# Batch 0 of an attention and channel-mix kernel in fp32 on TensorE, new planner costs, and one more tile in three rings

## The chip, the cores and the metric

The kernel runs on one core of a Trainium2 chip. A core has a matrix engine (TensorE, PE in the profile, with PEld for its weight loads), a vector engine (VectorE, DVE), an activation engine (ScalarE, ACT), a general engine (GpSimd, POOL), and a queue engine (SyncE, SP) that starts DMAs here. Each works through its own instructions in order and waits on semaphores. Data lie in SBUF, and matmuls write into eight PSUM banks. The metric is the time of one execution on the device in microseconds (us), as the median of several runs.

## The reference

```python
def _attn_ref(q, k, v, g_q, g_k):          # (8, 12, 448, 64) each
    q_n, k_n = (rmsnorm(q, g_q), rmsnorm(k, g_k))
    scores = 1.0 / np.sqrt(64) * np.matmul(q_n, k_n.transpose(0, 1, 3, 2))
    attn = np.exp(scores - np.max(scores, axis=-1, keepdims=True))
    attn = attn / (np.sum(attn, axis=-1, keepdims=True) + 1e-09)
    return np.matmul(attn, v)

def _moe_ref(x, mu_k, mu_r, w_k, w_v, w_r): # x (8, 448, 768), w_k 768x1024, w_v 1024x768, w_r 768x768
    xk = mu_k * x + (1.0 - mu_k) * x_prev   # x_prev: x moved by one token
    xr = mu_r * x + (1.0 - mu_r) * x_prev
    k = np.maximum(xk @ w_k, 0.0)
    return 1.0 / (1.0 + np.exp(-(xr @ w_r))) * (k * k @ w_v)
```

q, k, v and the result are fp32. The five weight inputs come as 64-bit floats.

## The kernel before

fp32 accuracy is had from f16 matmuls. Each operand is split into a high half (rounded to f16) and a low half (the rest, again in f16), and each product is three f16 matmuls: high x high, high x low, low x high.

**Attention.** Two heads make a pair, two pairs a unit `u`; a batch is 6 pairs or 3 units, and the tokens are 448 = 7 blocks of 64. `stats` (L568) and `preps` (L591) normalise q and k; for the first 6 units (`PE_T`) `turn` (L625) transposes them on PE as fp32 and ACT and DVE split the result into `stk`. `scores` (L709) runs over 7 groups per unit (168 in all): 6 groups of one pair and 128 tokens, and one corner group for the last 64 tokens of both pairs. A group writes two sc banks, one per head; the two heads stand in different halves of the array. `expo` (L744) finds the row maximum (DVE) and the exponential with its sum (ACT).

The probabilities then go one of two ways (`probs` L756, `probs_pe` L789). Ten groups, the odd ones below 21 (`PE_P`), go by PE: ACT writes the exponential to a `nat` tile as fp32, POOL scales it by 1/sum, PE transposes it as fp32 into sc banks, ACT copies out the high half and DVE the low half into `pT`. All others go by DMA: ACT and DVE split the scaled exponential straight out of the sc banks into a `nat` tile (`split` L813), and SP transposes that by DMA into `pT`. `attends` (L821) multiplies with v. `vprep` (L673) splits v into `vh` and `vl`, scaled by a power of two. `pT` has one place for even pairs and one for odd ones. The `nat` ring has 4 tiles; at the start it can borrow space in `xk`, which is why some `nat` tiles are named xk in the profile, and weight staging tiles kk.

**Channel mix.** `mix` (L871) makes xk and xr for a batch from 6 pairs (df on POOL, then DVE, split by ACT and POOL). `moe` (L992) then runs, per batch, the key products (mm<-xk with wk), squares them into `kk` (`square` L1051, ring kf), and the receptance and value products. `wload`, `weights` and `wsplit` (L896 to L931) bring in 20 weight tiles of 128 columns, decode them from 64-bit floats (POOL, ACT, DVE), find each column's scale through a product on PE and its diagonal (dg, DVE, and a true fp32 matmul with ones), and split them. Of batch 0, the key products may begin once all its pairs are mixed and all wk tiles are there, and the rest once all 20 tiles are done.

**The order.** All parts are generators that yield instructions. A list scheduler (`Plan.run` L300) holds a modelled clock for each engine, and takes the instruction with the earliest start less a priority. `Plan.emit` (L250) advances the clocks by modelled prices: `TR_COST` for a transposition on PE, constants for a DMA, and a rule that a DVE instruction with all operands in SBUF begins no sooner than 190 ns before POOL's last one ends. That order is the order on each engine; semaphores do the rest on the chip. A `Ring` (L329) hands out tiles of one shape.

All instructions are recorded by one helper (L256 in the profile), so groups are told apart by the tiles' names.

Of the kernel before, what the change touches and what calls it, by code (L numbers as in the profile page):

```python
# [74 lines left out]
Q_DVE = 1  # L75
PE_T = 6
SWITCH = 600
MODE = {"sc": 1, "t6": 2, "av": 3}
# [11 lines left out]
SC_KEEP = 2  # L90
TR_COST = 300
W_GAP = 10e3
# [4 lines left out]
DMA_SHARE = 1.0  # L97
PE_SLOW = 1.0
F64_EXP = 2.0 ** -112
F64_NEG = -2.0 ** 32  # L100
# [53 lines left out]
def in_psum(x):  # L154
    return "PSUM" in str(x.tensor.space)
# [37 lines left out]
class Plan:  # L193
    LAT = 35

    def __init__(self, tc):
        self.tc = tc
        self.clk = dict.fromkeys(("PE", "DVE", "ACT", "POOL", "SP"), 0.0)
        self.last, self.use, self.threads = {}, {}, []
        self.form, self.dma_free, self.pool_end, self.n = None, {"SP": 0.0, "ACT": 0.0}, 0.0, 0  # L200

# [48 lines left out]
    def emit(self, ops):  # L250
# [18 lines left out]
        elif ops[0].fn.__name__.startswith("dma"):  # L269
# [3 lines left out]
            if "transpose" in op.fn.__name__:  # L273
                w, iss, tot = n / 128 * 1.21, 1510, 4000
            else:
                w, iss, tot = n / 55, 600, 3300
            w, tot = w * DMA_SLOW, tot * DMA_SLOW
# [11 lines left out]
        else:  # L289
            op = ops[0]  # L290
            pace, dur = (x * OP_SLOW for x in price(op))
            if e == "DVE" and not any(in_psum(x) for x in op.kw.values() if isinstance(x, bass.AP)) and width(op.kw["out"]) > 2:
                s = max(s, self.pool_end - 190)
            self.clk[e] = s + pace
            if e == "POOL":
                self.pool_end = s + dur
            self.note(op, s + dur)
        self.n += 1

    def run(self):  # L300
        while self.threads:
            best, key = None, None
            for th in list(self.threads):
                if not isinstance(th[2], list):
                    if not th[2]():
                        continue
                    self.advance(th)
                    if th not in self.threads or not isinstance(th[2], list):
# [3 lines left out]
                wait = SWITCH if mode == 0 and self.form else 0  # L312
                k = max(self.clk[th[2][0].eng] + wait, th[3] + slack) - PS * (th[1]() if callable(th[1]) else th[1])
                if best is None or k < key:
                    best, key = th, k
# [13 lines left out]
class Ring:  # L329
    def __init__(self, pool, shape, dtype, name, n, plan):  # L330
        self.pool, self.shape, self.dtype, self.name, self.plan = pool, shape, dtype, name, plan
        self.free, self.of, self.lent = ["%s%d" % (name, k) for k in range(n)], {}, {}

# [11 lines left out]
    def get(self, early=False):  # L345
# [5 lines left out]
        if not isinstance(tag, str):  # L351
            self.of[id(tag)] = (tag, None, tag)
            return tag
        pool = self.pool() if callable(self.pool) else self.pool
        t = pool.tile(self.shape, self.dtype, name=tag, bufs=1)
# [33 lines left out]
def attn_moe_kernel(tc, q, k, v, g_q, g_k, mu_k, mu_r, w_k, w_v, w_r, out):  # L389
# [201 lines left out]
    def preps():  # L591
        for u in range(NQ):
# [4 lines left out]
            for n, t in enumerate(LD.pop(u)):  # L597
# [3 lines left out]
                if u < PE_T:  # L601
# [4 lines left out]
                    R["qk"].put(t)  # L606
                    yield from turn(w, X, n)
                    R["nat"].put(nat)
# [15 lines left out]

    def turn(w, X, n):  # L625
        for a0 in range(0, NT, 4):
# [14 lines left out]
            hi, lo = (X[:, n, o + a0:o + a0 + m, :] for o in (0, NT))  # L641
            if n == 0:
                yield A.activation(out=hi, in_=src, func=AF.Copy, scale=gc[:, 0:1])
# [21 lines left out]
    def vpreps():  # L665
        for i in range(NPAIR):
            st["vi"] = i
            yield from until(lambda: i in VF and st["tq"] >= GATE_V)
            vh = yield from R["vh"].get()
            vl = yield from R["vl"].get()  # L670
            yield from vprep(i, VF.pop(i), vh, vl)

    def vprep(i, vf, vh, vl):  # L673
# [4 lines left out]
        vs = small.tile([P, 2], F32, name="vs", bufs=4)  # L678
        yield A.activation(out=vh.bitcast(BF16), in_=vf, func=AF.Square, accum_out=vs[:, 0:1])
        pt = yield from banks["ot"].get()  # L680
        yield T.matmul(form=("v", 60), out=pt[:, 0:P], lhsT=vs[:, 0:1].bitcast(BF16)[:, 1:2].broadcast_to([P, P]), rhs=ident16, start=True, stop=True)
# [5 lines left out]
        yield V.tensor_scalar(out=iv.bitcast(I32), in0=sv.bitcast(I32), scalar1=-1.0, scalar2=float(0x7F000000), op0=ALU.mult, op1=ALU.add)  # L687
        yield A.activation(out=vh, in_=vf, func=AF.Copy, scale=sv)
        yield V.scalar_tensor_tensor(out=vl, in0=vf, scalar=sv, in1=vh, op0=ALU.mult, op1=ALU.subtract)
        VFREE.append(vf)  # L690
        VV[i] = vh, vl, iv
        if hp == NP - 1:
# [16 lines left out]
    def scores():  # L709
        for gi, (u, x, t0) in enumerate(groups):  # L710
            yield from until(lambda: u in TQ and len(banks["sc"].free) > (SC_KEEP if gi in PE_P else 1) and not st["zq"])
            tp = None
            if gi in PE_P:
                tp = yield from R["nat"].get(u < 3)
# [5 lines left out]
            both_pairs = t0 == NT - 1  # L720
            for m, (kl, ql) in enumerate(((0, 0), (0, 1), (1, 0))):
                for i in (2 * u + 1, 2 * u) if both_pairs else (2 * u + x,):
                    X = TQ[u]
                    for h in (1, 0):
# [3 lines left out]
                        ops.append(T.matmul(  # L728
                            form=("t6" if both_pairs else "sc", 3 * S / 2.368),
                            out=both[h][o:o + HD, 0:S] if both_pairs else both[h][:, 0:S],  # L730
                            lhsT=X[hs, 1, ql * NT + t0, o:o + HD] if both_pairs else X[hs, 1, ql * NT + t0 + i % 2, :],
                            rhs=X[hs, 0, kl * NT:(kl + 1) * NT, o:o + HD],
                            start=(m == 0), stop=(m == 2)))
            yield ops
# [21 lines left out]
    def probs(gi, both, sums, D, tp):  # L756
        u, x, t0 = groups[gi]
        yield from until(lambda: len(D) == 2 and st["g"] == gi)
        for i in (2 * u, 2 * u + 1) if t0 == NT - 1 else (2 * u + x,):
            if i not in PT:  # L760
                yield from until(lambda: PTFREE[i % 2])
                PTFREE[i % 2] = False
                PT[i] = PTQ[:, :, i % 2 * S:(i % 2 + 1) * S]
                CNT[i] = 0
# [24 lines left out]
    def probs_pe(u, x, t0, sums, tp):  # L789
# [8 lines left out]
        for a0 in range(0, NT, 4):  # L798
# [5 lines left out]
            src = z[:, 0:m * P].rearrange("p (a c) -> p a c", c=P)  # L804
            hi, lo = (PTQ[:, h + a0:h + a0 + m, c0:c0 + P] for h in (0, NT))
            yield A.copy(out=hi, in_=src)
            yield V.tensor_tensor(out=lo, in0=src, in1=hi, op=ALU.subtract)
            banks["sc"].put(z)
# [12 lines left out]
    def attends():  # L821
        for i in range(NPAIR):
# [5 lines left out]
            ops = []  # L828
            for j, (pl, hl, c) in enumerate(PASSES):
                for h in range(2):  # L830
                    ops.append(T.matmul(
                        form=("av", len(PASSES) * S / 2.368),
                        out=av[h * HD:(h + 1) * HD, 0:S],
                        lhsT=(vl if hl else vh)[:, NSL * h + c, :],
                        rhs=pT[:, NT * pl + (NSL - 1) * h + c, :],
                        start=(j == 0), stop=(j == len(PASSES) - 1)))
            yield ops
            PTFREE[i % 2] = True
            R["vh"].put(vh)
            R["vl"].put(vl)  # L840
            for lo, hi in ((0, NT),) if i % 2 == 0 else ((NT - 1, NT), (0, NT - 1)):
                o = 0 if i % 2 == 0 or lo else HD
                yield A.activation(out=x[:, 1 + lo:1 + hi, :].rearrange("p t c -> p (t c)"), in_=av[:, o:o + (hi - lo) * HD], func=AF.Copy, scale=iv)
            banks["ot"].put(av)
# [86 lines left out]
    def wsplit(nm, kt, c, ci, f):  # L931
# [178 lines left out]
```

## Time and profile before

| | |
|---|---|
| median of 3 runs | 1060.49 us (1059.37 to 1060.85) |
| the profiled execution, its own time | 1058.49 us |
| its span in the profile | 1056.7 us |
| PE busy | 925.9 us (88%), 6185 matmuls |
| DVE busy | 802.9 us (76%) |
| ACT busy | 770.7 us (73%) |
| POOL busy | 675.8 us (64%) |

The page cuts the span into 40 equal slices of 26.4 us; a digit is the busy share in tenths, PEclk the granted TensorE clock in tenths of full speed:

```profile
PE   1667666889988999998989999999899999999997
DVE  5888899898699688868997897959876898673100
PEclk9567878899999999999999999999999999999999
```

PE is at 60 to 70% in the slices of the first 180 us, at a reduced clock, and near full from then on. DVE is at 80 to 90% from the second slice. In rows of instruction groups, the numbers behind the bar are busy us and mean ns of one, then the idle time of the engine just before them and what ended it. An instruction's row begins with its start and its length in us.

### The profile page before, as it was taken

The numbers are of one execution on the slowest core, as the hardware profiler recorded it, in microseconds if no ns is written. First come the engines' busy times: TensorE is split into PE (matmuls) and PEld (weight loads), VectorE is DVE, ScalarE is ACT, GpSimd is POOL, SyncE is SP. The second block draws the span as 40 slices with busy tenths as digits, with TensorE's granted clock in tenths as the row PEclk, the third lists the DMA queues.
The fourth block names the chain that finished last, engine by engine and source line by source line (L and its number), as shares of the span: only waits on it lengthen the run. The fifth ranks groups of instructions, "written<-read, shape, count | busy, mean of one in ns | idle before, by whom it ended". The sixth has DMA issues, their size and how long they took to land. (4 is left out here: it accounts for less than half of the span.)

```text
span 1056.7 us, 19126 instructions
## 1 busy us (share of the span) xinstructions
PE 925.9 (88%) x6185; PEld 488.9 (46%) x6185; DVE 802.9 (76%) x2034; ACT 770.7 (73%) x1786; POOL 675.8 (64%) x716
## 2 busy tenths in 40 slices
PE   1667666889988999998989999999899999999997
PEld 1334323444544555454534455455445554455564
DVE  5888899898699688868997897959876898673100
ACT  3687877888679788877788787868787888773311
POOL 2575579655588576874698457857695569725711
PEclk9567878899999999999999999999999999999999
DMA  6865557876877899778976998679887898753011
GB/s 172 196 145 123 136 140 189 176 145 134 178 134 146 163 172 165 155 149 148 176 160 129 181 174 165 136 143 183 151 152 153 165 179 164 135 89 79 1 31 30
DMA packets 467108, 151.68 MB, mean 144 GB/s; under 512 B 438848, under 2 KB 463424, under 8 KB 467008
## 3 DMA queue, kind: packets, MB, share of 16 engines
q1 hardware_dynamic: 447472, 132.47, 66.1%
q10 hardware_dynamic: 19536, 18.00, 5.9%
q8 instruction: 48, 0.79, 0.3%
q14 instruction: 52, 0.43, 0.1%
HBM read 50.40 MB, written 11.01 MB: 58 GB/s over the span
## 5 line engine op out<-in xcount | busy, mean ns | idle before, releaser
L256 PE MATMUL mm<-wvh,kk 128*128 128x384 f16 x896 | 233.3, 326 | 0.5 <-DVE o L256 0.5
L256 ACT ACTIVATE sc<-sc,sums 128x448 f32<-128x448 f32 x316 | 192.2, 611 | 54.1 <-DVE sums L256 47.1
L256 DVE SCALAR_TENSOR_TENSOR nat<-sc,sums,nat 128x448 f16<-128x448 f32 x306 | 199.8, 676 | 37.0 <-ACT nat L256 35.3
L256 PE MATMUL mm<-xk,wkh 128*128 128x448 f16 x768 | 213.1, 359 | 9.7 <-DVE WSC L256 5.7
L256 ACT ACTIVATE nat<-sc,sums 128x448 f16<-128x448 f32 (+1 forms) x326 | 194.9, 646 | 25.8 <-DVE sums L256 10.4
L256 DVE TENSOR_REDUCE sums<-sc 128x1 f32<-128x448 f32 x336 | 193.6, 614 | 21.9 <-PE sc L256 21.3
L256 PE MATMUL mm<-wrh,xr 128*128 128x384 f16 x672 | 177.1, 326 | 0.0
L256 PEld LDWEIGHTS <-kk 128*128 128x128 f16 (+1 forms) x1362 | 129.5, 98 | 97.2 <-issue 15.6
L256 PE MATMUL sc<-stk 64*128 64x448 f16 (+1 forms) x1152 | 128.3, 369 | 34.4 <-DVE nat L256 19.4
L256 PE MATMUL mm<-wvl,kk 128*128 128x384 f16 x448 | 146.0, 326 | 0.0
L256 PE MATMUL mm<-xk,wkl 128*128 128x448 f16 x384 | 137.8, 359 | 0.0
L256 PE MATMUL ot<-pT,vh 128*64 128x448 f16 x768 | 122.4, 376 | 17.3 <-DMA pT<-nat 8.0
L256 PEld LDWEIGHTS <-xr 128*128 128x128 f16 x1008 | 95.6, 98 | 73.4 <-issue 13.1
L256 DVE SCALAR_TENSOR_TENSOR df<-x,bsc,df 128x448 f32<-128x448 f32 x96 | 108.3, 1137 | 25.3 <-POOL df L256 25.0
L256 PEld LDWEIGHTS <-wkh 128*128 128x128 f16 x768 | 72.8, 99 | 83.9 <-issue 25.5
L256 PE MATMUL mm<-wrl,xr 128*128 128x384 f16 x336 | 109.5, 326 | 0.0
L256 PEld LDWEIGHTS <-stk 64*128 64x128 f16 (+1 forms) x1152 | 43.5, 99 | 103.3 <-issue 68.5
L256 POOL TENSOR_TENSOR o<-o,bsc 128x384 f32<-128x384 f32 x48 | 43.8, 913 | 69.5 <-DVE o L256 57.0
L256 POOL TENSOR_TENSOR nat<-nat 128x448 f32<-128x448 f32 x46 | 53.9, 1171 | 50.6 <-ACT nat L256 45.4
L256 POOL TENSOR_TENSOR qk<-qk,ss 128x896 f32<-128x896 f32 x36 | 62.5, 1737 | 34.5 <-DVE ss L256 28.8
L256 DVE SCALAR_TENSOR_TENSOR o<-o,mm 128x384 f32<-128x384 f32 x56 | 30.6, 546 | 70.2 <-PE mm L256 70.2
L256 POOL TENSOR_TENSOR nat<-qk,nat 128x896 f16<-128x896 f32 x36 | 67.8, 1883 | 23.4 <-ACT nat L256 23.3
(141 smaller groups left out, 1632.6 us busy)
## 6 DMA issues: line engine op xcount, KB each, us to landing
out_dram<-o SPq DMA_DIRECT2D x56, 192.0 KB, 3.3
qk<-in_k_dram SPq DMA_DIRECT2D x46, 224.0 KB, 4.0
qk<-in_q_dram SPq DMA_DIRECT2D x108, 64.0 KB, 2.5
vf<-in_v_dram SPq DMA_DIRECT2D x96, 64.0 KB, 2.8
raw<-in_moe_w_v_dram ACTq DMA_DIRECT2D x12, 512.0 KB, 4.7
vf<-in_v_dram SPq DMA_DIRECT2D x96, 48.0 KB, 2.5
raw<-in_moe_w_r_dram ACTq DMA_DIRECT2D x12, 384.0 KB, 3.7
kk<-in_moe_w_k_dram ACTq DMA_DIRECT2D x8, 384.0 KB, 4.0
```

What stands on the lines that cost most here:

```text
L256: r = op.fn(op.kw["out"], op.kw["value"]) if op.fn.__name__ == "memset" else op.fn(**op.kw)
```

## The change

Four things change.

1. For the first three units (`U32 = 3`, which is batch 0) nothing is split. q, k, probabilities and v stay fp32, and each product is one fp32 matmul instead of three f16 ones. `whole` views a tile of two f16 halves as one fp32 tile. All 21 score groups of these units go by PE, so there are 11 more by PE and 11 fewer by DMA. The copies out of PSUM after a transposition go to ACT or DVE, whichever has the earlier modelled clock. v is used as it was loaded, but `vprep` still finds its scale, since the mix needs it.
2. Because `pT` now changes its format, pair 6 waits until both its places are free.
3. The planner: `TR_COST` 130 for 300, `ACC_GAP` 130 between accumulating ACT instructions, dearer DMA issues, and a rule on sharing between DVE and POOL that holds both ways.
4. After the weight staging pool is closed, the rings kf, df and nat get one tile more each (`LATE_BUFS`; kfx, dfx and natx in the rows). Two guards in `wsplit` make steps wait until values exist.

```diff
-TR_COST = 300
+U32 = 3
+TR_COST = 130
+ACC_GAP = 130
+LATE_BUFS = (("kf", 1), ("df", 1), ("nat", 1))
+def whole(ap):
+    c = ap.shape[-1]
+    return ap.rearrange("p a c -> p (a c)").bitcast(F32).rearrange("p (a c) -> p a c", c=c)
...
-                w, iss, tot = n / 128 * 1.21, 1510, 4000
+                w, iss, tot = n / 128 * 1.21, 1600, 4000
...
+            if e == "ACT":
+                acc = op.kw.get("accum_out") is not None
+                if acc and self.acc:
+                    s = max(s, self.clk[e] + ACC_GAP)
+                self.acc = acc
+            if e == "POOL" or e == "DVE" and not any(in_psum(x) for x in op.kw.values() if isinstance(x, bass.AP)) and width(op.kw["out"]) > 2:
+                for a, b in self.held["DVE" if e == "POOL" else "POOL"]:
+                    if a <= s < b - 190:
+                        s = b - 190
...
+            for name, n in LATE_BUFS:
+                R[name].grow(late_pool[0], n)
...
+            if u < U32:
+                dst = whole(X[:, n])[:, a0:a0 + m, :]
+                if plan.clk["ACT"] < plan.clk["DVE"]:
+                    yield A.activation(out=dst, in_=src, func=AF.Copy, scale=gc[:, 0:1]) if n == 0 else A.copy(out=dst, in_=src)
...
-            yield from until(lambda: u in TQ and len(banks["sc"].free) > (SC_KEEP if gi in PE_P else 1) and not st["zq"])
+            yield from until(lambda: u in TQ and len(banks["sc"].free) > (SC_KEEP if u < U32 or gi in PE_P else 1) and not st["zq"])
             tp = None
-            if gi in PE_P:
+            if u < U32 or gi in PE_P:
...
-            for m, (kl, ql) in enumerate(((0, 0), (0, 1), (1, 0))):
+            terms = ((0, 0),) if u < U32 else ((0, 0), (0, 1), (1, 0))
+            for m, (kl, ql) in enumerate(terms):
...
-                yield from until(lambda: PTFREE[i % 2])
+                yield from until(lambda: PTFREE[i % 2] and (i != 2 * U32 or PTFREE[1]))
...
+            if u < U32:
+                dst = whole(PTQ[:, :, :])[:, a0:a0 + m, c0:c0 + P]
+                yield A.copy(out=dst, in_=src) if plan.clk["ACT"] < plan.clk["DVE"] else V.tensor_copy(out=dst, in_=src)
+            else:
...
+            passes = [(0, 0, c) for c in range(NSL)] if vl is None else PASSES
...
+            yield from until(lambda: st["mus"])
...
+            yield from until(lambda: st.get("rsc"))
```

Three places show how the order moves. The first is PE at the first two score groups of the kernel (stk0 holds q and k of unit 0, sc are the banks; an fp32 matmul has no separate weight load). Before, from the last transposition of k and q into the first group:

```order
L256 LDWEIGHTS kk0_103
L256 MATMUL ot0_251<-kk0_103 128x128
L256 MATMUL sc3_274<-ident_70,nat3_230 128x2x64 x2
L256 MATMUL sc3_274<-ident_70,nat3_230 128x128
L256 LDWEIGHTS stk0_195
L256 MATMUL sc0_287<-stk0_195 128x448
L256 LDWEIGHTS stk0_195
```

and now both groups:

```order
L265 MATMUL sc0_251<-stk0_193 128x448
L265 MATMUL sc4_250<-stk0_193 128x448
L265 MATMUL sc2_263<-stk0_193 128x448
L265 MATMUL sc1_262<-stk0_193 128x448
L265 MATMUL ot0_225<-dg_234,ones_87 128x128
```

A group is six matmuls with six weight loads before, and two matmuls now.

The second place is DVE in batch 0, before, around the third group's maxima (sums2), and now, around the sixth's and seventh's (sums5, sums0):

```order
L256 TENSOR_SCALAR sums1_106<-sums1_106 128x2
L256 TENSOR_SCALAR WIN_82<-WSC_81 128x1
L256 RECIPROCAL sums1_106<-sums1_106 128x2
L256 SCALAR_TENSOR_TENSOR nat1_321<-sc4_286,sums0_105,nat1_321 128x448
L256 TENSOR_REDUCE sums2_107<-sc1_381 128x1
L256 TENSOR_REDUCE sums2_107<-sc2_382 128x1
L256 SCALAR_TENSOR_TENSOR stk1_348<-sc3_384,gc_80,stk1_348 128x384
L256 SCALAR_TENSOR_TENSOR nat1_321<-sc0_287,sums0_105,nat1_321 128x448
```

```order
L265 TENSOR_REDUCE sums5_110<-sc4_515 128x1
L265 TENSOR_REDUCE sums5_110<-sc2_516 128x1
L265 COPY pT_102<-sc3_521 128x4x128
L265 TENSOR_SCALAR sums5_110<-sums5_110 128x2
L265 RECIPROCAL sums5_110<-sums5_110 128x2
L265 COPY pT_102<-sc1_528 128x4x128
L265 TENSOR_REDUCE sums0_105<-sc4_542 128x1
L265 TENSOR_REDUCE sums0_105<-sc3_543 128x1
L265 COPY pT_102<-sc1_559 128x4x128
```

The low halves nat and stk are gone, and plain copies into pT stand between the maxima.

The third place is PE around the diagonal product (dg) of the last weight tile, before and now:

```order
L256 MATMUL mm1_2384<-xk0_104,wkl_89 128x448
L256 MATMUL sc0_2446<-ident_70,nat0_2443 128x128 x4
L256 MATMUL mm0_2399<-dg_2425,ones_87 128x128
L256 LDWEIGHTS wkh_88
L256 MATMUL mm1_2471<-xk0_104,wkh_88 128x448
```

```order
L265 LDWEIGHTS wkl_89
L265 MATMUL mm1_2366<-xk0_104,wkl_89 128x448
L265 MATMUL mm0_2361<-dg_2376,ones_87 128x128
L265 LDWEIGHTS vs_2217
L265 MATMUL ot0_2394<-ident16_75,vs_2217 128x128
L265 LDWEIGHTS wkh_88
```

The key products come in eight tiles of 18, and mm1_2384 is the sixth, mm1_2366 the eighth. Before, 108 of them stand ahead of this dg on PE, and 228 score matmuls; now 138, and 90 f16 and 48 fp32 score matmuls.

More of the change, by code (lines that the diff above doesn't have):

```diff
@@ L199, in __init__ @@
         self.last, self.use, self.threads = {}, {}, []
-        self.form, self.dma_free, self.pool_end, self.n = None, {"SP": 0.0, "ACT": 0.0}, 0.0, 0
+        self.form, self.dma_free, self.acc, self.n = None, {"SP": 0.0, "ACT": 0.0}, False, 0
+        self.held = {"DVE": [], "POOL": []}
     def margin(self, form):
@@ L291, in emit @@
             pace, dur = (x * OP_SLOW for x in price(op))
-            if e == "DVE" and not any(in_psum(x) for x in op.kw.values() if isinstance(x, bass.AP)) and width(op.kw["out"]) > 2:
-                s = max(s, self.pool_end - 190)
+            if e == "ACT":
[7 more added lines that the diff above has]
+                        s = b - 190
+                h = self.held[e]
+                h.append((s, s + dur))
+                del h[:-16]
             self.clk[e] = s + pace
-            if e == "POOL":
-                self.pool_end = s + dur
             self.note(op, s + dur)
@@ L312, in run @@
                 wait = SWITCH if mode == 0 and self.form else 0
+                if self.acc and th[2][0].eng == "ACT" and th[2][0].kw.get("accum_out") is not None:
+                    wait += ACC_GAP
                 k = max(self.clk[th[2][0].eng] + wait, th[3] + slack) - PS * (th[1]() if callable(th[1]) else th[1])
@@ L331, in __init__, with grow @@
         self.pool, self.shape, self.dtype, self.name, self.plan = pool, shape, dtype, name, plan
-        self.free, self.of, self.lent = ["%s%d" % (name, k) for k in range(n)], {}, {}
+        self.free, self.of, self.lent, self.more = ["%s%d" % (name, k) for k in range(n)], {}, {}, {}
+    def grow(self, pool, n):
+        for _ in range(n):
+            tag = "%sx%d" % (self.name, len(self.more))
+            self.more[tag] = pool
+            self.free.append(tag)
     def lend(self, owner, views):
@@ L353, in get @@
             return tag
-        pool = self.pool() if callable(self.pool) else self.pool
+        pool = self.more.get(tag) or (self.pool() if callable(self.pool) else self.pool)
         t = pool.tile(self.shape, self.dtype, name=tag, bufs=1)
@@ L606, in preps @@
                     R["qk"].put(t)
-                    yield from turn(w, X, n)
+                    yield from turn(w, X, n, u)
                     R["nat"].put(nat)
@@ L623, in preps, with turn @@
             st["tq"] = u + 1
-    def turn(w, X, n):
+    def turn(w, X, n, u):
         for a0 in range(0, NT, 4):
@@ L668, in vpreps @@
             yield from until(lambda: i in VF and st["tq"] >= GATE_V)
+            if i < 2 * U32:
+                yield from vprep(i, VF.pop(i), None, None)
+                continue
             vh = yield from R["vh"].get()
@@ L678, in vprep @@
         vs = small.tile([P, 2], F32, name="vs", bufs=4)
-        yield A.activation(out=vh.bitcast(BF16), in_=vf, func=AF.Square, accum_out=vs[:, 0:1])
-        pt = yield from banks["ot"].get()
+        if vh is None:
+            pt = yield from banks["ot"].get()
+            yield A.activation(out=pt.rearrange("p (a c) -> p a c", c=HD), in_=vf, func=AF.Square, accum_out=vs[:, 0:1])
+        else:
+            yield A.activation(out=vh.bitcast(BF16), in_=vf, func=AF.Square, accum_out=vs[:, 0:1])
+            pt = yield from banks["ot"].get()
         yield T.matmul(form=("v", 60), out=pt[:, 0:P], lhsT=vs[:, 0:1].bitcast(BF16)[:, 1:2].broadcast_to([P, P]), rhs=ident16, start=True, stop=True)
@@ L720, in scores @@
             both_pairs = t0 == NT - 1
-            for m, (kl, ql) in enumerate(((0, 0), (0, 1), (1, 0))):
+            terms = ((0, 0),) if u < U32 else ((0, 0), (0, 1), (1, 0))
+            for m, (kl, ql) in enumerate(terms):
                 for i in (2 * u + 1, 2 * u) if both_pairs else (2 * u + x,):
                     X = TQ[u]
+                    K_, Q_ = (whole(X[:, n]) if u < U32 else X[:, n] for n in range(2))
                     for h in (1, 0):
@@ L760, in probs @@
             if i not in PT:
[L761 removed]
+                yield from until(lambda: PTFREE[i % 2] and (i != 2 * U32 or PTFREE[1]))
                 PTFREE[i % 2] = False
[L763 removed]
+                PT[i] = (whole(PTQ[:, :, :]) if u < U32 else PTQ)[:, :, i % 2 * S:(i % 2 + 1) * S]
                 CNT[i] = 0
@@ L804, in probs_pe @@
             src = z[:, 0:m * P].rearrange("p (a c) -> p a c", c=P)
-            hi, lo = (PTQ[:, h + a0:h + a0 + m, c0:c0 + P] for h in (0, NT))
-            yield A.copy(out=hi, in_=src)
-            yield V.tensor_tensor(out=lo, in0=src, in1=hi, op=ALU.subtract)
+            if u < U32:
+                dst = whole(PTQ[:, :, :])[:, a0:a0 + m, c0:c0 + P]
+                yield A.copy(out=dst, in_=src) if plan.clk["ACT"] < plan.clk["DVE"] else V.tensor_copy(out=dst, in_=src)
+            else:
+                hi, lo = (PTQ[:, h + a0:h + a0 + m, c0:c0 + P] for h in (0, NT))
+                yield A.copy(out=hi, in_=src)
+                yield V.tensor_tensor(out=lo, in0=src, in1=hi, op=ALU.subtract)
             banks["sc"].put(z)
```

41 lines of the change are left out of this document (25 added, 16 removed).

## The prediction

> **What bounds the kernel now.** I read the stretches of the trace first, cut where the kernel changes character: until all six pairs of batch 0 are mixed (165 us), until the last of the 20 weight tiles is scaled (223.5 us), and on to the end. The columns are the stretch, its length, busy time and count of PE, PEld (weight loads), DVE, ACT and POOL, then the granted clock, DMA share and GB/s.
>
> ```profile
> 0.00:165.00 165.00, 94.14 (x574) 51.68 (x575) 136.91 (x417) 113.94 (x253) 95.50 (x123) 0.75 0.64 153
> 165.00:223.50 58.50, 44.72 (x282) 23.23 (x281) 53.09 (x131) 47.59 (x100) 42.37 (x44) 0.89 0.81 179
> 223.50:250.00 26.50, 24.34 (x179) 12.42 (x178) 22.69 (x67) 22.62 (x51) 12.22 (x14) 1.00 0.61 119
> 250.00:965.00 715.00, 676.67 (x4651) 352.25 (x4649) 577.22 (x1405) 565.13 (x1333) 489.77 (x496) 1.00 0.82 155
> 965.00:1050.00 85.00, 85.00 (x501) 48.89 (x500) 12.39 (x18) 21.45 (x51) 35.08 (x38) 1.00 0.07 19
> ```
>
> From 223.5 us on PE is the bound: 676.7 of 715 us busy at full clock, then 85 of 85. Up to 223.5 us (I call this the head) it is not: PE is busy 138.9 us, idle 84.6 us, at a clock of 0.75 and 0.89. There DVE is the fullest engine, 136.9 + 53.1 = 190.0 of 223.5 us, and ACT has 161.5. The change's arithmetic lies in the head, so the question is how much earlier the head ends, and how much PE work is then left. What PE idled for ahead of instructions on the score banks (sc) in the first 165 us (total, times):
>
> ```profile
>   DVE nat L256: 9.4, 5
>   ACT nat L256: 9.3, 5
>   DVE pT L256: 5.3, 4
>   DVE xk L256: 2.7, 3
> ```
>
> These are 26.7 us of waits for a bank that is being split into f16 halves (xk is a probability tile in borrowed space), the steps that the change removes for batch 0.
>
> **The change, on DVE.** I counted each kind of DVE row up to the diagonal product (dg) of the last weight tile, which starts at 222.4 us. The view of DVE's instructions on the score banks in this stretch (min/median/max ns):
>
> ```profile
> L256 DVE SCALAR_TENSOR_TENSOR nat<-sc,sums,nat x33: 664/675/684, 39.4 to 222.8; 128x448 f16<-128x448 f32 x33
> L256 DVE TENSOR_SCALAR sums<-sc x23: 143/152/160, 34.5 to 223.4; 128x2 f32<-128x2 f32 x23
> L256 DVE TENSOR_TENSOR pT<-sc,pT x20: 537/616/692, 43.7 to 143.8; 128x512 f16<-128x512 f32 x10, 128x384 f16<-128x384 f32 x10
> L256 DVE SCALAR_TENSOR_TENSOR stk<-sc,gc,stk x10: 604/678/751, 22.5 to 184.8; 128x512 f16<-128x512 f32 x5, 128x384 f16<-128x384 f32 x5
> L256 DVE TENSOR_TENSOR stk<-sc,stk x10: 543/614/683, 26.9 to 196.3; 128x512 f16<-128x512 f32 x5, 128x384 f16<-128x384 f32 x5
> L256 DVE SCALAR_TENSOR_TENSOR xk<-sc,sums,xk x10: 667/676/685, 59.2 to 136.4; 128x448 f16<-128x448 f32 x10
> ```
>
> and three other groups (busy, mean ns of one, idle before it):
>
> ```profile
> L256 DVE TENSOR_REDUCE sums<-sc 128x1 f32<-128x448 f32 x66 | 39.2, 615 | 6.0 <-PE sc L256 5.8
> ...
> L256 DVE SCALAR_TENSOR_TENSOR vl<-vf,bstat,vh 128x512 f16<-128x512 f32 x9 | 9.1, 1017 | 0.7 <-ACT vh L256 0.7
> ...
> L256 DVE TENSOR_SCALAR sums<-sums 128x2 f32<-128x2 f32 x10 | 2.8, 276 | 0.7 <-ACT nat L256 0.5
> ```
>
> Removed ahead of that point: 20 low halves of probabilities (nat, xk) at 0.676 = 13.5; 20 low halves after transposition (pT) at 0.616 = 12.3; 6 of v (vl) at 1.017 = 6.1; 10 of q and k (stk), four at 0.678 and six at 0.614 = 6.4. Together 38.3 us. Added: 21 plain copies pT and 6 plain copies stk. No large DVE copy stands in the trace. The price lies between the fixed part (the small row at 0.152, so 27 x 0.152 = 4.1 us) and that of the same width with two operands (16 of 512 columns at up to 0.69 and 11 of 384 at 0.54 = 17.0 us). The one-operand reduction, 615 ns for 448 columns, is not cheaper per column, so I take 17.0. Also added: 11 sums rows at 0.276 for 10 at 0.152, 1.5; and two more reductions each of sums and of squares, pulled forward from later work, 4 x 0.61 = 2.4. Net -17.4.
>
> Rows overlap on DVE, so fewer of them save a little less:
>
> ```profile
> 220.12 1.28 DVE L256 SCALAR_TENSOR_TENSOR wvl<-wf,WSC,wvh 128x1024 f16<-128x1024 f32 x1
> 221.33 1.15 DVE L256 TENSOR_REDUCE sums<-sc 128x1 f32<-128x448 f32 x2
> ```
>
> The first is 1.28 long, but the next starts after 1.21: 0.07 us each, and 26 rows fewer, 1.8. DVE has **15.6 us less** to do in the head. With its idle time kept as it is, the head is shorter by that.
>
> ACT loses as well (20 high halves, 6 of v, a part of the copies that DVE takes over); it had more room than DVE, so it does not set the end. POOL gains 22 scalings of probabilities:
>
> ```profile
> L256 POOL TENSOR_SCALAR nat<-nat,sums 128x448 f32<-128x448 f32 x20 | 13.1, 664 | 10.4 <-DVE sums L256 8.7 <-DVE stm L256 1.5
> ```
>
> 22 x 0.664 = 14.6 us on top of 137.9 in the head, so 152 of about 208: hidden beside DVE's work. If that cover is gone, weight decoding (raw) and tile scaling (wf), queued behind these scalings on POOL, come late by up to these 14.6 us, and DVE waits for them (rival 2). One row shows a price of sharing:
>
> ```profile
> L256 DVE SCALAR_TENSOR_TENSOR df<-x,bsc,df 128x448 f32<-128x448 f32 x12 | 13.5, 1136 | 2.1 <-POOL df L256 2.0
> ```
>
> df, with two tensors in SBUF, takes 1.136 us where nat, as wide but with one of them in PSUM, takes 0.675. The Trainium skill, "SBUF — State Buffer", section "Who interferes with whom", says that a DVE instruction with two SBUF inputs and a GpSimd instruction that reads SBUF exclude each other for their whole length. By that rule the added scalings could hold up each df of the head once more, at most 12 x 0.46 = 5.5 us, which would make the sum below 1050 instead of 1045.
>
> Eleven of 158 transpositions of probabilities by DMA go too, and with them their place in SP's queue; PE's waits before 165 us name none of them, so I give nothing for them.
>
> **The wait that is added.** pT changes from fp32 to f16 after pair 5, so the first write of pair 6 waits for the attention of pair 5, not of pair 4. Their starts now:
>
> ```profile
> 133.93 0.58 PE L256 MATMUL ot<-pT,vh 128*64 128x448 f16 x2
> ...
> 151.07 0.58 PE L256 MATMUL ot<-pT,vh 128*64 128x448 f16 x2 [3.56 <-DVE bstat L256]
> ```
>
> The write could be late by up to 17.1 us, and behind it stand on SP the loads of later q, k and v. But probabilities come out in order, so that group stands behind the last of pair 5 anyway, and the attention of pair 5 needs just that one: I expect the attention's own 4 us, while PE has the first key products to do. Nothing on the path, with 17.1 as the other end. The guards on mus and rsc ask for values that the order has long before; nothing.
>
> **The change, on PE.** Starts of neighbouring rows give the pace. A score group of six, then key products:
>
> ```profile
> 197.44 0.74 PE L256 MATMUL sc<-stk 64*128 64x448 f16 x6
> 198.11 0.55 PE L256 MATMUL mm<-xk,wkh 128*128 128x448 f16 x2
> 198.50 0.35 PE L256 MATMUL mm<-xk,wkl 128*128 128x448 f16 x1
> ```
>
> An f16 pass over 448 columns takes 0.19 us (two in 0.39); the group takes 0.67, so two halves of the array run side by side (six in turn would be 1.1). Attention times v, 24 matmuls, and a corner group of twelve:
>
> ```profile
> 211.63 0.38 PE L256 MATMUL ot<-pT,vh 128*64 128x448 f16 x2
> ...
> 214.02 0.76 PE L256 MATMUL sc<-stk 64*64 64x448 f16 x12
> ```
>
> 2.39 us for the first; the corner is no longer than a group of six (0.76 to 0.74), 0.70. Seven fp32 transpositions, and the only true fp32 matmul, dg, one instruction in two records:
>
> ```profile
> 126.34 0.93 PE L256 MATMUL sc<-ident,nat 128*128 128x128 f32 x7
> 127.11 0.22 PE L256 MATMUL ot<-ident,vs 128*128 128x128 bf16 x1
> ...
> 193.85 0.39 PE L256 MATMUL mm<-dg,ones 128*128 128x128 f32 x2
> 194.08 0.22 PE L256 MATMUL ot<-ident,vs 128*128 128x128 bf16 x1
> ```
>
> 0.11 us a transposition; 0.23 us for 128 columns of fp32, so 448 take 0.80. **Unknown** is whether two fp32 matmuls on halves of the array also run side by side. If they do nearly so, a score group of two is 1.2, a corner of four 1.6, attention times v (eight) 3.6; if not, 1.6, 3.2 and 6.4. Over batch 0 (18 groups, 3 corners, 6 pairs) that is +9.5, +2.7 and +7.3 = 19.5 us, or +16.7, +7.5 and +24.1 = 48.3 us. The 77 further transpositions are 8.5 us. So PE has 28 to 57 us more at full clock, against 84.6 us of idle time. I take 28, as the f16 rows on halves are the nearest, and keep 57 for the range.
>
> This is hidden by idle time only if it waits for little. At the measured clocks the 138.9 busy us are about 109 at full speed; 109 + 28 = 137 in 208 us is a share of 0.66 even at full clock. DVE's reductions already wait 5.8 us for PE's scores; each group of batch 0 now comes 0.5 us later at full clock and more at less, and transpositions stand in PE's queue ahead of the next scores. For this I add **6 us** to the head, as much again as this wait.
>
> **What comes ahead.** In the new order 138 of the key products (mm<-xk) stand before the last tile's dg, not 108, and one score group more: 30 x 0.19 + 0.67 = **6.3 us less** PE work in the part that PE bounds.
>
> **The rings and the planner.** kf, df and nat get one tile more after the head. What they can save is bounded by PE's idle time between 250 and 965 us, 38.3 us, of which these rows (total, times, longest) name what a nat tile touches:
>
> ```profile
> PE sc L256 <- DVE nat L256: 13.9, 24, 1.8
> PE ot L256 <- DMA pT<-nat: 7.7, 9, 1.9
> ```
>
> The planner's new costs redraw the whole order, which can lose as well as win; between -12 and +8 us I take 0.
>
> **Sum**, against the profiled execution's own 1058.49 us (span 1056.7): -15.6 - 6.3 + 6 = -15.9, so 1042.6. The median of the runs shown, 1060.49, is 2.0 higher; by it I say **1045**.
>
> **The rivals.**
> 1. PE becomes the bound of the head (slower). fp32 halves run in turn: 109 + 57 = 166 us at full clock. At the granted clock of the old head (0.79 over its 223.5 us) that is 210 us, plus the first 20 us in which PE has almost nothing, and some 10 of its 38 us of other waits (84.6 - 26.7 - 20): 240, so 17 us later instead of 15.6 earlier; less the 6.3 ahead, 1060.5 + 11 = 1071. Against it: PE got a better clock when busier (0.89 at 76% busy, 0.75 at 57%); at 0.95 the same work is 175, the head 205 and the rival gone. It decides where PE takes 223.5 + 6.3 - 30 = 200 us: from 158 us of full-clock work at 0.79, from 190 at 0.95. The Trainium skill, "TensorE: Matmul & The Clock Gate", section "Part 4: PE-mode transpose", says that transpositions do not count as PE being busy, so the full clock is not granted for them. By that rule the 77 more would not lift the clock, and this rival would stand. The row at 126.34 shows seven at full speed, but behind matmuls, so it does not exclude the rule.
> 2. The head is not DVE's. If loading, decoding and scaling on POOL set the pace of the weight tiles, or the pT wait bites, the head ends where it did, and only the 6.3 us ahead remain: 1054; with more waits for POOL up to 1060, no change.
> 3. The tiles in the rings take 12 of the 38.3 us of idle time as well, 1033; with copies at the low price 13 us less on DVE, 1032 by itself.
>
> **How the numbers follow.** Forecast 50% (own range 1034 to 1055); rival 1 20% (1063 to 1072); rival 2 13%, half of it within 0.2%; rival 3 17% (1025 to 1034). The range from 1027 to 1067 leaves out the ends of rivals 1 and 3. What a measurement can tell from no change is about 0.2%, 2 us. Faster: 50 + 17 + 6 = 73%; same 7%; slower 20%.
>
> **What would show it.** The last dg should start near 213 us, with DVE busy some 174 us up to there; score groups of two should take 1.2 us at full clock, not 1.6; PE's clock in the head should exceed 0.8, and its waits for DVE nat, ACT nat, DVE pT and DVE xk should be gone from batch 0. From 250 to 965 us PE should stay at 94 to 95%. If PE waits for POOL nat instead, or idle time past the head differs by over 10 us, a step of this is wrong.

## Result and profile after

The changed kernel takes a median of **1051.33 us** (1048.6 to 1055.12, 6 runs), and the kernel before, on the same chip, 1060.67 us (1059.37 to 1064.51, 6 runs). The ratio is 0.9909, with a 95% interval of 0.9891 to 0.9927: 9.3 us faster. The profiled execution took 1048.6 us with a span of 1046.8, so 9.9 us less than the one of before (1056.7).

The page after, busy time by engine, and the same three lines of the 40 slices (26.2 us each) as before:

```profile
PE 937.4 (90%) x6166; PEld 491.6 (47%) x6166; DVE 796.4 (76%) x2001; ACT 747.2 (71%) x1753; POOL 686.5 (66%) x738
...
PE   1678685788999999999999999999899999999997
...
DVE  4888868997988688968987888879876887884100
...
PEclk9788876999999999999999999999799999999999
```

PE has 11.5 us more busy time than before (925.9) and the span is 9.9 shorter, so 21.4 us of PE's idle time went. Where it went, the windows show (columns as in the prediction). Before:

```profile
0.00:250.00 250.00, 163.20 (x1032) 87.32 (x1033) 212.69 (x611) 184.16 (x403) 150.09 (x181) 0.81 0.68 155
250.00:960.00 710.00, 671.67 (x4611) 349.55 (x4609) 576.70 (x1405) 564.38 (x1331) 488.67 (x493) 1.00 0.83 156
```

and after, with the head cut as in the prediction as well:

```profile
0.00:165.00 165.00, 104.58 (x561) 56.50 (x561) 126.23 (x386) 93.98 (x215) 106.70 (x143) 0.85 0.46 124
165.00:223.50 58.50, 43.68 (x281) 21.78 (x282) 52.50 (x125) 49.56 (x105) 45.26 (x48) 0.84 0.88 186
...
0.00:223.50 223.50, 148.26 (x842) 78.29 (x843) 178.74 (x510) 143.54 (x319) 151.96 (x190) 0.85 0.57 140
...
0.00:228.60 228.60, 152.20 (x867) 80.39 (x868) 183.37 (x518) 148.64 (x332) 155.94 (x193) 0.85 0.57 138
...
0.00:250.00 250.00, 168.95 (x975) 89.32 (x976) 199.28 (x568) 162.93 (x364) 160.55 (x201) 0.86 0.56 135
...
250.00:960.00 710.00, 687.28 (x4718) 355.94 (x4717) 583.15 (x1418) 564.38 (x1343) 490.68 (x499) 0.99 0.83 156
```

Up to 250 us PE does 5.75 us more work in as much less idle time. From 250 to 960 us its idle time falls from 38.3 to 22.7 us: **15.6 of these 21.4 us lie past the head**, where the arithmetic is the same in both kernels. The head did not get shorter. The last tile's diagonal product on DVE began at 222.4 us, and now (min/median/max ns, first and last start):

```profile
L265 DVE TENSOR_TENSOR dg<-mm,ident x12: 277/280/292, 97.4 to 228.6; 128x128 f32<-128x128 f32 x12
```

6.2 us later. Starts of some landmarks on PE, read from the two traces (us):

| | before | after |
|---|---|---|
| first key product of batch 0 | 162.5 | 175.9 |
| last key product of batch 0 | 232.5 | 231.7 |
| first receptance product of batch 0 | 235.7 | 240.8 |
| first key product of batch 1 | 300.0 | 305.3 |
| ... of batch 2 | 422.5 | 420.6 |
| ... of batch 4 | 652.4 | 638.0 |
| ... of batch 7 | 969.0 | 959.1 |
| last value product | 1050.7 | 1040.8 |

The change is 5 us behind at batch 1, nearly level at batch 2, and 8 to 14 us ahead from batch 4 on. What PE waits for between 250 and 960 us (total, times, longest), before, beside the two rows of the prediction:

```profile
PE ot L256 <- ACT vh L256: 6.9, 5, 2.8
```

and after:

```profile
PE ot L265 <- ACT vh L265: 12.0, 11, 3.2
PE sc L265 <- DVE nat L265: 5.2, 6, 2.1
PE ot L265 <- DMA pT<-natx: 2.0, 2, 1.1
PE ot L265 <- DMA pT<-nat: 1.8, 2, 0.9
```

Waits for DVE nat fell from 13.9 to 5.2 us, for the transposing DMAs from 7.7 to 3.8; waits for ACT's square of v (vh) rose from 6.9 to 12.0.

### The profile page after: what moved, and what is told of

Same layout as the page of the kernel before. It is cut to its first block, busy times and chain, and to the rows that moved or that the text cites. A ratio compares the mean times of both kernels' runs of the same rounds, so it can differ in the third digit from the quotient of the medians.

```text
span 1046.8 us, 18947 instructions
## 1 busy us (share of the span) xinstructions
PE 937.4 (90%) x6166; PEld 491.6 (47%) x6166; DVE 796.4 (76%) x2001; ACT 747.2 (71%) x1753; POOL 686.5 (66%) x738
## 5 line engine op out<-in xcount | busy, mean ns | idle before, releaser
L265 ACT ACTIVATE sc<-sc,sums 128x448 f32<-128x448 f32 x294 | 181.3, 618 | 43.8 <-DVE sums L265 40.4
L265 ACT ACTIVATE nat<-sc,sums 128x448 f16<-128x448 f32 (+1 forms) x258 | 157.3, 650 | 26.4 <-DVE sums L265 18.8
L265 DVE SCALAR_TENSOR_TENSOR nat<-sc,sums,nat 128x448 f16<-128x448 f32 x228 | 148.7, 675 | 21.9 <-ACT nat L265 21.7
L265 PE MATMUL sc<-stk 64*128 64x448 f16 (+3 forms) x1104 | 132.8, 386 | 11.7 <-DVE nat L265 7.5
L265 PE MATMUL ot<-pT,vh 128*64 128x448 f16 x672 | 101.9, 360 | 4.8 <-DMA pT<-natx 2.0
L265 POOL TENSOR_TENSOR qk<-qk,ss 128x896 f32<-128x896 f32 x36 | 63.8, 1773 | 34.2 <-DVE ss L265 31.0
L265 ACT ACTIVATE o<-mm,bsc 128x128 f32<-128x128 f32 x144 | 45.3, 382 | 56.6 <-PE mm L265 44.2
L265 POOL TENSOR_TENSOR nat<-qk,nat 128x896 f16<-128x896 f32 x30 | 57.3, 1911 | 28.2 <-ACT nat L265 28.1
L265 DVE SCALAR_TENSOR_TENSOR df<-x,bsc,df 128x448 f32<-128x448 f32 x68 | 64.8, 962 | 10.6 <-POOL df L265 10.5
```

The costliest lines, as they stand in the source:

```text
L265: r = op.fn(op.kw["out"], op.kw["value"]) if op.fn.__name__ == "memset" else op.fn(**op.kw)
```

## The experiments

Two questions were open: what sets the head's length, if not DVE, and which part of the change shortened the stretch past it. All medians are beside the kernel before on the same chip (1061.29, 1061.52 and 1060.14 us in the three sets of runs). "Old costs" means the planner of before: `TR_COST` 300, `ACC_GAP` 0, the old DMA constants and the one-way sharing rule. Every kernel here computes the full result.

### The pace of the weight tiles

The weight steps' priority in the scheduler holds a pace, which I had not used when I predicted: 10 us for each finished tile.

```python
    def wprio():
        return PRIO_W + (BOOST_W if st["want"] == "w" else 0) + (plan.now() - W_START - W_GAP * st["wdone"]) * W_PUSH
```

`pace_8500` changes that number alone:

```diff
-W_GAP = 10e3
+W_GAP = 8.5e3
```

> The changed kernel with the planner's pace for weight tiles at 8.5 us instead of 10 us. If that pace sets the head, 19 intervals of 1.5 us less bring the last dg from 228.6 to about 200 us, and the time falls by some 5 to 12 us, to 1039 to 1046. If DVE, POOL and PE's chain in batch 0 set it, the last dg moves by less than 8 us and the time stays within 4 us of 1051.

Measured: 1081.57 us (1080.09 to 1084.11), ratio 1.0189 (1.016 to 1.0217). Its diagonal products, its windows and PE's waits from 250 to 960 us:

```profile
L265 DVE TENSOR_TENSOR dg<-mm,ident x12: 270/278/293, 89.0 to 206.8; 128x128 f32<-128x128 f32 x12
```

```profile
0.00:223.50 223.50, 147.33 (x851) 79.17 (x852) 181.91 (x516) 141.88 (x314) 151.81 (x191) 0.86 0.53 133
250.00:960.00 710.00, 656.97 (x4438) 332.64 (x4435) 567.29 (x1401) 557.02 (x1320) 477.21 (x484) 0.96 0.84 154
```

```profile
PE sc L265 <- DVE nat L265: 19.0, 14, 5.6
PE ot L265 <- ACT vh L265: 12.8, 14, 2.2
```

The last dg starts 21.8 us earlier (206.8), with DVE doing 3.2 us more within 223.5 us, and the first receptance product 11.4 us earlier (229.4). So DVE had room, and in the changed kernel the planner's pace set most of the head's end: it moved by 21.8 of the 28.5 us (19 x 1.5) that the shorter pace could give. The pace was not moved in the kernel before. Yet the kernel is 30 us slower than the change, where it was expected to be faster: batch 3 begins at 550.9 us for 518.5, and PE idles 53.0 us between 250 and 960. A shorter head did not carry to the end.

### One part, and two parts, of the change

```diff
fp32_only        TR_COST, ACC_GAP, DMA constants, sharing rule: old; -LATE_BUFS of three +LATE_BUFS = ()
planner_only     -U32 = 3  +U32 = 0;  +LATE_BUFS = ()
rings_only       -U32 = 3  +U32 = 0;  costs: old
fp32_and_costs   +LATE_BUFS = ()
fp32_and_rings   costs: old
costs_and_rings  -U32 = 3  +U32 = 0
```

> Batch 0 in fp32 alone, with the old planner costs and no more tiles in the rings. If fp32 brought the gain (fewer splits on DVE and ACT), the time is 1048 to 1054 us. If the weight tiles are paced by the planner's own rule of one tile per 10 us (W_GAP), the last dg stays between 218 and 230 us, DVE only idles more in the head, and the time is within 4 us of before, 1057 to 1064.

> The new planner costs alone, all batches in f16 halves, no more tiles. If a truer order brought the gain, 1050 to 1055 us, with PE's idle time between 250 and 960 us down from 38 to about 25 us. If the rings or fp32 did, 1058 to 1064.

> One more kf, df and nat tile alone, old planner costs, all batches in f16 halves. If the spare tiles brought the gain, 1050 to 1055 us, with PE's waits for DVE nat between 250 and 960 us down from 13.9 to about 6 us, and the head as before (last dg at 222 us). If not, 1058 to 1064.

> The changed kernel without the three more tiles. If the rings carry the gain, 1060 to 1066 us, with PE waiting 12 us or more for DVE nat between 250 and 960 us; if not, 1050 to 1055; scatter: 1050 to 1075.

> The changed kernel with the old planner costs. If the costs carry the gain, 1060 to 1070 us; if not, 1050 to 1055; scatter: 1050 to 1075. Over all kernels with and without fp32 the means tell whether fp32 is worth anything: level, or better by over 5 us.

> New costs and rings, but batch 0 in f16 halves: the changed kernel without fp32. If fp32 is what makes the difference, 1058 to 1066 us; if the costs and the rings together do, 1050 to 1055; if orders just scatter, anything from 1050 to 1075.

| | median, us | ratio to before (95%) | last dg, us | PE idle 250 to 960, us |
|---|---|---|---|---|
| before | | 1 | 222.4 | 38.3 |
| fp32_only | 1068.61 | 1.0083 (1.0054 to 1.0112) | 244.3 | 38.1 |
| planner_only | 1065.80 | 1.0044 (1.0027 to 1.0061) | 232.9 | 35.8 |
| rings_only | 1075.40 | 1.0134 (1.0100 to 1.0168) | 225.2 | 48.8 |
| fp32_and_costs | 1080.91 | 1.0187 (1.0159 to 1.0215) | 233.8 | 45.6 |
| fp32_and_rings | 1079.88 | 1.0185 (1.0156 to 1.0215) | 241.8 | 42.5 |
| costs_and_rings | 1067.89 | 1.0073 (1.0053 to 1.0093) | 235.2 | 42.3 |
| after (all three) | 1051.33 | 0.9909 (0.9891 to 0.9927) | 228.6 | 22.7 |

Each part alone and each pair is slower than before; only the three together are faster. The parts do not add up. Five of the six medians (all but `costs_and_rings`) lie above every range expected for them. `fp32_only` also speaks on the head: the first 223.5 us of it are

```profile
0.00:223.50 223.50, 145.75 (x795) 77.36 (x796) 165.22 (x481) 137.22 (x304) 150.78 (x186) 0.85 0.52 129
```

with DVE at 165.2 us, 25 less than before, and the last dg 22 us later, where 218 to 230 us were expected if the pace sets it. So the pace is not alone: at the same 10 us the last dg lies between 222 and 244 us in the kernels of this table. In `rings_only` the waits past the head take another shape:

```profile
PE ot L265 <- ACT vh L265: 17.4, 13, 4.2
PE sc L265 <- DVE nat L265: 14.6, 18, 3.6
```

The same arithmetic past the head gives 36 to 53 us of idle time in these six kernels and `pace_8500`, where the order of the change gives 22.7. That raised a new theory: the gain belongs to one particular order, not to any part.

### Neighbours: numbers that should not matter

Four kernels move the modelled price of a transposition by 3 to 8%, two around the change and two around the kernel before:

```diff
after_tr120    -TR_COST = 130   +TR_COST = 120
after_tr140    -TR_COST = 130   +TR_COST = 140
before_tr290   -TR_COST = 300   +TR_COST = 290
before_tr310   -TR_COST = 300   +TR_COST = 310
```

> The changed kernel with one planner number nudged: a transposition on PE is priced 120 instead of 130. No instruction, tile or byte differs, only the order. If the gain belongs to the three parts (fp32, costs, rings) working together, this stays at 1047 to 1055 us. If it belongs to the one order that came out, it falls elsewhere by up to 1 to 2%, 1045 to 1075, with the head about the same (last dg 220 to 240 us) and PE's idle time between 250 and 960 us anywhere from 23 to 50 us.

> The same nudge the other way, 140 instead of 130. Parts together: 1047 to 1055 us. One order: 1045 to 1075, not the same as with 120.

> The kernel before with the transposition priced 290 instead of 300; again only the order differs. If orders scatter by themselves, it lies between 1055 and 1080 us and not within 2 us of before; if the order is robust, within 4 us of 1061.

> The kernel before with 310 instead of 300. If orders scatter by themselves, between 1055 and 1080 us; if robust, within 4 us of 1061. With the nudged ones of the changed kernel it also tells whether the two families differ: fp32 and the rest are worth something on the mean only if the nudged changed kernels are on average faster than the nudged kernels of before by more than their scatter.

Measured, 10 runs each:

| | median, us | ratio to before (95%) | last dg, us | PE idle 250 to 960, us |
|---|---|---|---|---|
| after_tr120 | 1061.67 | 0.9998 (0.9978 to 1.0018) | 232.3 | 36.6 |
| after_tr140 | 1064.24 | 1.0020 (1.0001 to 1.0040) | 231.2 | 34.2 |
| before_tr290 | 1072.53 | 1.0086 (1.0059 to 1.0113) | 240.6 | 38.2 |
| before_tr310 | 1067.14 | 1.0042 (1.0022 to 1.0062) | 228.0 | 41.3 |

By the ratios, a nudge costs the change 9 to 12 us and the kernel before 4 to 9 us (6 to 11 by its medians). The nudged changes lose past the head, where they idle 34 to 37 us for 22.7; `before_tr290` idles there as the kernel before does, and its last dg comes 18 us later. Of the scheduled orders that ran, both originals are the fastest of their kind. A kernel that was kept because its order came out fast would look like this; how the two were found is not known here.

### A nudge only past the head

`late_nudge` adds 10 ns to the 600 that the scheduler allows most of the attention's steps on PE, from the last weight tile on:

```diff
-        return MARGIN_V if form == "v" else MARGIN
+        return MARGIN_V if form == "v" else MARGIN + (10 if self.st["wdone"] == 20 else 0)
```

> The changed kernel with one planner number nudged only after the last weight tile (a matmul's slack 610 instead of 600); PE's order is the same row for row over the first third. If the time is decided by the head, it stays within 3 us of 1051. If the order behind the head is worth several us by itself, it comes out elsewhere, 1045 to 1065, with the same last dg (228 to 229 us) and the difference all in PE's idle time after some 350 us.

Measured: 1087.8 us (1086.4 to 1091.21), ratio 1.0265 (1.0239 to 1.0292), the slowest of all and beyond the 1045 to 1065 that were expected. In the two traces PE's matmuls come in the same sequence, by kind of tile, for the first 2462 of 6166 records, up to 471 us, and the last dg lies within 2 us (230.4). Windows of the change, then of `late_nudge`:

```profile
520.00:600.00 80.00, 77.77 (x527) 39.89 (x521) 65.72 (x151) 63.80 (x151) 58.92 (x57) 1.00 0.82 151
600.00:700.00 100.00, 97.44 (x662) 51.23 (x663) 82.12 (x199) 78.74 (x185) 73.40 (x74) 1.00 0.84 161
700.00:960.00 260.00, 248.56 (x1698) 128.14 (x1697) 206.56 (x497) 199.72 (x479) 167.42 (x177) 0.97 0.80 149
```

```profile
520.00:600.00 80.00, 75.94 (x517) 38.81 (x519) 65.01 (x156) 64.32 (x151) 57.54 (x57) 1.00 0.83 157
600.00:700.00 100.00, 81.72 (x504) 41.36 (x501) 62.16 (x150) 64.45 (x146) 68.26 (x66) 0.88 0.68 136
700.00:960.00 260.00, 235.84 (x1611) 119.29 (x1610) 207.87 (x509) 202.29 (x479) 160.49 (x168) 0.95 0.78 145
```

From 520 to 600 us they are nearly alike; then PE loses 15.7 us of work in 100 us, and 12.7 more up to 960; its idle time from 250 to 960 us is 51.9 us. From 600 to 700 us in `late_nudge`, the timeline on PE, on ACT and on SP's queue (start, length, in brackets the idle time before it and what ended it):

```profile
633.55 0.33 PE L265 MATMUL mm<-wvh,kk 128*128 128x384 f16 x1
642.95 0.29 PE L265 MATMUL ot<-ident,vs 128*128 128x128 bf16 x1 [9.08 <-ACT vh L265]
...
658.83 1.30 PE L265 MATMUL sc<-stk 64*128 64x448 f16 x6 [5.93 <-DVE nat L265]
```

```profile
637.46 0.95 ACT L265 ACTIVATE natx<-qk 128x896 f32<-128x896 f32 x1 [5.73 <-DMA qk<-in_q_dram]
642.18 0.63 ACT L265 ACTIVATE vh<-vf 128x512 bf16<-128x512 f32 x1 [3.76 <-DMA vf<-in_v_dram]
```

```profile
632.09 3.75 SPq L265 DMA_DIRECT2D qk<-in_q_dram  x5
635.88 1.25 SPq L265 DMA_DIRECT2D qk<-in_k_dram  x2
637.18 1.88 SPq L265 DMA_DIRECT2D out_dram<-o  x3
639.11 9.03 SPq L265 DMA_DIRECT2D vf<-in_v_dram  x9
```

Read from the bottom: the loads of v stand in SP's queue behind seven loads of q and k and three stores of results, and start at 639.1. ACT waits for a load of q, then for the first of v, and squares v at 642.2. PE's next instruction is the small matmul (0.29 us) that sums those squares for v's scale; it waits 9.08 us, and PE takes its matmuls in order. Behind it stand 24 matmuls of attention that wait 1.57 us more for the split of v, and a later score group waits 5.93 us for DVE's nat. The Trainium skill, "TensorE: Matmul & The Clock Gate", section "Why this matters for your kernels", advises against idle gaps of over about 3 us between bursts of matmuls, since the clock falls after them. The trace agrees for this gap: the granted clock is 1.00 up to it and 0.50 behind it, and 0.88 over the 100 us, where the change has 1.00.

```profile
643.00:650.00 7.00, 5.14 (x25) 2.06 (x26) 5.62 (x18) 4.49 (x10) 3.58 (x5) 0.50 0.19 43
```

In the change only two gaps past 300 us exceed 2 us (2.07 and 3.15), in `late_nudge` eight do, in the kernel before three. Why the order of the change escapes the gap of 9 us is not shown.

## Why the prediction was right, and where it was not

The direction and the range held (1051 in 1027 to 1067), and the forecast of 15.9 us was too large by 6. But that was luck: the head, for which the gain was forecast, ended 6.2 us later, and the time fell in the range through a term that was taken as 0.

1. **The step that failed** is "With its idle time kept as it is, the head is shorter by that." DVE did get less to do: 190.0 to 178.7 us in the first 223.5. Up to its last dg it had 188.9 us to do before and 183.4 now, not the 174 of the forecast, and idled 33.5 us before and 45.2 now (228.6 - 183.4). An engine that is 85% busy was taken for the bound, while the pace of the tiles in the planner set most of the end, as `pace_8500` shows for the changed kernel. So the head's part of rival 2 was right: it is not DVE's. The rival named loading, decoding and scaling on POOL as the cause; the cause shown, for most of it and in the change, is the pace. That POOL's scalings come in addition is seen (137.9 to 152.0 us), but not as what set the end.
2. **The 6.3 us of work ahead** were hardly worth it. From the last dg to the first receptance product it took 13.3 us before and 12.2 now: 1.1 us. Before, PE worked through the rest of the key products from 223.5 us up to the first receptance product without a gap. Now it ran out of them, and most of what was saved became a wait, again of the small matmul for v's scale, which stands right ahead of that product:

```profile
240.78 0.23 PE L265 MATMUL ot<-ident,vs 128*128 128x128 bf16 x1 [4.64 <-ACT vh L265]
```

   The planner also orders the receptance products behind all 20 tiles; which of the two would have held them without this wait is not shown.
3. **The added waits** (6 us, as much again as DVE's reductions waited for PE's scores) came in another place. The reductions wait no longer than before (5.8 us, now 5.2); it is the new copies that wait for PE's transpositions. DVE's waits up to 228.6 us:

```profile
DVE pT L265 <- PE sc L265: 9.3, 8, 3.8
...
DVE sums L265 <- PE sc L265: 5.2, 8, 1.4
```

   The first key product comes 13.4 us later, and from 0 to 165 us PE now waits for POOL's scaling, as the last part of the prediction allowed:

```profile
PE sc L265 <- POOL nat L265: 8.5, 5, 2.6
PE sc L265 <- DVE nat L265: 5.9, 2, 4.6
...
PE sc L265 <- DVE pT L265: 3.3, 6, 0.8
...
PE sc L265 <- ACT nat L265: 1.4, 3, 0.7
```

   The four old waits shrank or went (26.7 us to 10.6 for nat on DVE and ACT and pT; xk is gone), and the wait for POOL rose from 2.5 to 8.5 us.
4. **fp32 on PE** was mis-sized, on the safe side. The prediction took 1.2 us for a score group of two, 1.6 for a corner and 3.6 for attention times v. Starts of neighbouring rows in the change (records are double, two for each fp32 matmul):

```profile
120.55 1.02 PE L265 MATMUL sc<-stk 64*128 64x448 f32 x4
121.50 0.55 PE L265 MATMUL sc<-ident,nat 128*128 128x128 f32 x3
...
77.65 0.98 PE L265 MATMUL sc<-stk 64*64 64x448 f32 x8
78.56 0.52 PE L265 MATMUL ot<-wf 128*128 128x128 bf16 x6
...
60.49 3.23 PE L265 MATMUL ot<-pT,vf 128*64 128x448 f32 x16
63.65 1.02 PE L265 MATMUL sc<-stk 64*128 64x448 f32 x4
```

   0.95, 0.91 and 3.16 us. Over batch 0 that is 18 x 0.28 + 3 x 0.21 + 6 x 0.77 = 10.3 us more than f16, not 19.5; with the transpositions 18.8 for 28. The prediction's own f16 rows, as shares of the same matmuls in turn (0.67 of 1.14, 0.70 of 2.28 and 2.39 of 4.56 us), would have given 0.94, 0.98 and 3.35. Rival 1 fell with it: halves run side by side, and PE's clock in the head rose from 0.79 to 0.85 as the forecast asked. The rule that transpositions do not count as PE being busy, from the Trainium skill, "TensorE: Matmul & The Clock Gate", section "Part 4: PE-mode transpose", did not show: 77 more transpositions went with a higher clock, but PE was busier as a whole (138.9 to 148.3 us in the first 223.5), so no run here decides on it.
5. **Copies** on DVE cost what the high end said (the line below). The further hold-up of df by POOL, up to 5.5 us, did not come: up to the last dg the 12 df took 0.99 us each, for 1.136 before. The five wvl, with two tensors in SBUF as well, took 1.72 for 1.41; why is not shown.

```profile
L265 DVE COPY pT<-sc 128x512 f32<-128x512 f32 (+1 forms) x21 | 13.2, 634 | 9.4 <-PE sc L265 9.3
```

6. **The rings and the planner**, taken at 0 between -12 and +8, gave what the kernel gained: 15.6 us less idle time past the head, outside the bound. The prediction's own test said that a change of over 10 us there makes a step wrong. But it is not a gain of the rings, as rival 3 had it: with f16 halves in batch 0 (`costs_and_rings`) the same rings and costs are 7.7 us slower than before, and with the rings alone 14 us.

Six kernels with fp32 in batch 0 and without the change's exact order (fp32_only, after_tr120, after_tr140, late_nudge, fp32_and_costs, fp32_and_rings) have a mean of 1073.9 us (1075.0 with `pace_8500`), and five without fp32 beside the kernel before 1069.7. So fp32 in batch 0 is not shown to be worth anything by itself. What is shown is that the 9.3 us hang on the order found with exactly these numbers. Over all 14 kernels the ratio to before follows PE's idle time from 250 to 960 us (correlation 0.89) and not the start of the last dg (-0.05). What makes that order good beyond its shorter waits for DVE's nat and the transposing DMAs stays open, as does whether fp32 would pay under an order that doesn't scatter; neither was tried. No version faster than the change was found.

## What to carry to other kernels

Where a scheduler redraws the whole order, time a few neighbours of both kernels, with numbers moved that should not matter, before a gain of 1% is put down to an edit: here they scatter from 1061 to 1088 us. Before a nearly full engine is called the bound of a stage, look for a rule in the planner that paces the stage, and move that rule alone. Past the head, look first for small instructions that stand at the front of an in-order queue and wait for a late load; one of 0.3 us waited 9 us here.

## What the runs showed of the hardware

Two fp32 matmuls of 448 columns on halves of the array take 0.95 us together, where one alone is estimated at 0.80 (from 128 columns in 0.23), and four on quarters take 0.91, all at a granted clock of 1.00: in fp32 the parts run side by side nearly in full. After the gap of 9.08 us on PE the granted clock was 0.50 up to 650 us, and pairs of attention matmuls began 0.37 us apart, for 0.19 at full clock. After the gap of 4.64 us in the change it was 0.50 from 242 to 244 us. So such a stall costs more than its own length. The length of the gap does not decide it alone: after 2.07 us at 733.2 in the change the clock was 0.50 as well, and after 2.82 us at 753.4 in the kernel before it stayed at 1.00.
